# A Fourier mixing layer feeding a mixture of experts: earlier zeroing and sign multiplies, and result scatters queued separately

## The chip, the cores and the metric

The kernel runs on one core of a Trainium2 chip. A core has five engines with one instruction queue each: TensorE (PE in the profile; its weight loads are PEld), VectorE (DVE), ScalarE (ACT), GpSimd (POOL) and SyncE (SP), and 16 DMA engines that move data between the device memory and the core's own memory. An engine takes its instructions in order, and one that waits for a semaphore holds up all that stand behind it in its queue. The metric is the time of one execution on the device in microseconds (us); smaller is better.

## The reference

```python
# x: (8, 2496, 256), filt_r and filt_i: (1249, 256)
X = np.fft.rfft(x, axis=1)
Y = X * (filt_r + 1j * filt_i)[None]
x = np.fft.irfft(Y, n=2496, axis=1).reshape(19968, 256)
logits = x @ w_gate                       # (19968, 8)
expert_idx = np.argmax(logits, axis=1)
probs = softmax(logits)                   # with 1e-9 added to the sum
gate_w = probs[np.arange(N), expert_idx]
for e in range(8):                        # each token goes to one expert
    h = np.maximum(x_of_e @ w1[e], 0.0)   # 256 -> 1024
    y_of_e = h @ w2[e]                    # 1024 -> 256
out = gate_w[:, None] * y                 # in the tokens' own order
```

All is in float32.

## The kernel before, in words

**The Fourier stage.** 2496 is 39 times 64, so a transform is one of length 39 (products with the table `tas`, called stage a), one of length 64 (`tbs`, stage b), a product with the filter `ht`, and the same two backwards (`tcs`, stage c, and `tds`, stage d). A batch is loaded in six chunks of up to four columns (`fin<-in_x`). Stage a's result `zo` goes to the device memory (`zd`) and comes back in another layout (`fin<-zd`); stage c's result `uo` does the same through `ud`. Batch 0 alone is turned on TensorE with transposes (`first_a`, `turn_z`, `first_c`, `turn_u`), without that detour. In `stage_b` VectorE makes three products per pair of frequencies (`ys`, and `yw` in two halves), and for batch 0 and part of the next ones GpSimd adds `yw` to `ys`; otherwise VectorE does.

**The filter and its signs.** `load_filters` loads `ht` in five chunks of four frequencies. The imaginary parts of a chunk are still to be multiplied by signs (`sgs`), on GpSimd. `turn_z` (line 624) issues these multiplies when it reaches a chunk, and has ScalarE copy the real parts to the other half of the partitions.

**The gates.** `logits` or `block_logits` multiply by the gate weights, which lie spread over larger tiles `wg` and `wb` whose other places are zero: `load_rest` (line 435) zeroes each on VectorE and then loads the weights over it from SyncE's queue.

**Routing.** `route` (line 734) finds each token's expert, gate value and place in a list of rows sorted by expert, mostly with small VectorE operations. GpSimd then copies the gate value beside the token's row in `yo`, and `scatter` (line 852) writes 117 rows with one indirect DMA to the table `rows` in the device memory. The tile of `rs`, which holds the gate values, has one buffer, so the next route's `rs` waits until GpSimd has copied the last gate value. `tile_map` (line 866) cuts the list into tiles of rows of one expert.

**The experts.** For a tile of 512, 256 or 128 rows, SyncE loads the rows (`xg`, `ng`) and the two halves of the expert's weights (`w1t`, `w2t`). VectorE transposes the rows. For the larger tiles the first product is done with seven block products in place of eight, for which GpSimd makes sums of weights (`w1_sums`, four operations) and of rows (`turn_x`, four operations). `result` (line 1069) makes 128 rows of the second product from 8 accumulated matmuls, multiplies by the gate on VectorE or ScalarE into one of four `ys` buffers, and has GpSimd write the rows to their places in `out` with an indirect DMA.

**What sets the order.** A class `Order` passes every instruction on and keeps estimated times for each engine while the program is built (`count`, line 178). A loop at the end picks the next piece of TensorE work: a Fourier step, or a product of the experts, whichever is estimated to be ready, in a set proportion. After each pick `flush` (line 490) issues the stores whose data are estimated to be ready, `more_loads` and `prefetch` issue loads, and `side` issues pieces of routing. So an edit that moves an estimate can move other instructions as well. Each engine's order is fixed when the program is built; the semaphore waits are put in by the tile library from reads and writes of the same tile. All instructions go through one line of `Order`, line 243, so the profile names nearly all of them L243, and they are told apart by their tiles.

Of the kernel before, what the change touches and what calls it, by code (L numbers as in the profile page):

```python
# [12 lines left out]
U32 = mybir.dt.uint32  # L13
# [111 lines left out]
class Order:  # L125
# [5 lines left out]
    def __init__(self, nc):  # L131
        self.nc = nc
        self.t = dict.fromkeys(("tensor", "vector", "scalar", "gpsimd", "sync", "transfers"), 0.0)
        self.slow = self.busy = self.last = 0.0
        self.lands = [0.0] * 8
        self.done, self.used, self.slots, self.ahead = {}, {}, {}, {}
        self.tensor, self.vector, self.scalar, self.gpsimd, self.sync = (
            Issue(self, name) for name in ("tensor", "vector", "scalar", "gpsimd", "sync"))
# [37 lines left out]
        return size / n * packet / 14e3 * (1.7 if n >= 1024 and (in_ if out.space == DRAM else out).ap[0][1] <= 64 else 1.0)  # L176

    def count(self, engine, op, args, named):
        aps = [a for a in list(args) + list(named.values()) if isinstance(a, bass.AP)]
        if not aps:  # L180
            return
        out, ins = aps[0], aps[1:]
        if "out" in named:
            out = named["out"]
            ins = [a for a in aps if a is not out]
        if op.endswith("value_load"):
            out, ins = None, aps
        at = named.get("out_offset")
        if at is not None:
            ins.append(at.ap)  # L190
        kept = [a for a in ins if a.space != DRAM or a.name[:2] in ("zd", "ud")]
        free = self.t[engine]
        start = max([free] + [self.ready(a) + (self.HOP if engine != "sync" else 0.0) for a in kept])
        if out is not None:
            start = max(start, self.ahead.pop(out.name, 0.0))
            n = int(np.prod([d[1] for d in out.ap][1:])) if out.space != DRAM else 0
        tail = 0.0
        if op.endswith("dma_start"):
            busy = 1.03 if engine == "gpsimd" else 0.4
            if engine == "sync":  # L200
                start = max(start, self.lands[-8])
            self.t[engine] = start + busy
            took = self.transfer(out, named["in_"])
            self.t["transfers"] = max(self.t["transfers"], start + busy) + took
            end, tail = self.t["transfers"], self.LOAD
            if engine == "sync":
                self.lands = self.lands[-7:] + [end + tail]
        else:
            if out is None:
                took = 0.8 if engine == "sync" else 0.02  # L210
            elif engine == "tensor":
                if start > self.busy + 1.2:
                    self.slow = start + 3.4
                rows = out.ap[0][1]
                took = max(0.1, 0.00085 * n) if op == "transpose" else max(0.216, 0.00169 * n) if rows > 32 else 0.00045 * n
                took *= 2.0 if start < self.slow else 1.0
                tail = 0.25
            elif engine == "vector":
                took = 0.15 + n / 960
            elif engine == "scalar":  # L220
                took = 0.16 + n / 1200
            else:
                took = 0.2 + n / 480
            end = self.t[engine] = start + took
            if engine == "tensor":
                self.busy = end
        for a in kept:
            self.used[a.name] = max(self.used.get(a.name, 0.0), end)
        for key in self.parts(out) if out is not None else ():
            self.done[key] = max(self.done.get(key, 0.0), end + tail)  # L230
        self.last = end + tail
# [59 lines left out]
def kernel(  # L291
# [16 lines left out]
    nc = Order(tc.nc)  # L308
# [39 lines left out]
    tau0 = perm.tile([1, 32], F32, name="tau0")  # L348
# [17 lines left out]
    wg = cst.tile([P, DH, CT], F32, name="wg")  # L366
    wb = cst.tile([P, NJ, CT], F32, name="wb")
# [29 lines left out]
    t = nc.t  # L397
# [17 lines left out]
    signs = []  # L415
# [18 lines left out]

    def load_rest():
        nc.sync.dma_start(out=tds, in_=td)
        nc.vector.memset(wg, 0.0)
        nc.sync.dma_start(out=wg[:, :, :E], in_=moe_w_gate.rearrange("(i p) e -> p i e", p=P))
        nc.vector.memset(wb, 0.0)
        for i in range(4):  # L440
            nc.sync.dma_start(out=wb[i * CT:(i + 1) * CT, :, i * E:(i + 1) * E], in_=moe_w_gate.rearrange("(j p) e -> p j e", p=CT))
        nc.sync.dma_start(out=ids0, in_=ids)
        nc.sync.dma_start(out=vld, in_=valid)

    def make_constants():
        make_identity(nc.nc, ident)
        nc.gpsimd.memset(ones, 1.0)
        nc.gpsimd.affine_select(
            out=tri, in_=ones, compare_op=ALU.is_gt, fill=0.0, base=0, pattern=[[1, P]], channel_multiplier=-1
        )  # L450
        nc.gpsimd.memset(msk, 0.0)
        for i in range(4):
            at = slice(i * CT, (i + 1) * CT)
            nc.gpsimd.tensor_copy(sel[at], ident[at, at])
            nc.gpsimd.memset(msk[at, i:i + 1], 1.0)
        nc.gpsimd.memset(seg, 1.0)
        nc.gpsimd.memset(seg[:, :, 0:1], 0.0)
        nc.gpsimd.memset(tot, 0.0)
        nc.gpsimd.iota(prow, pattern=[[0, 1]], base=0, channel_multiplier=1)
        nc.gpsimd.iota(tau_i, pattern=[[1, 32]], base=0, channel_multiplier=0)  # L460
        nc.vector.tensor_copy(tau0, tau_i)
        nc.gpsimd.iota(e_i, pattern=[[1, E]], base=0, channel_multiplier=0)
        nc.vector.tensor_scalar(em8, in0=e_i, scalar1=-float(E), scalar2=None, op0=ALU.add)
        nc.vector.tensor_scalar(eoff, in0=e_i, scalar1=float(TE), scalar2=None, op0=ALU.mult)
        nc.vector.tensor_copy(cnt, eoff)
        nc.vector.tensor_copy(done, eoff[0:1, :])
        nc.vector.memset(one, 1.0)
# [11 lines left out]
    NIN, YB = 7, 6  # L479
    sb.live["in"] = lambda: {tile.name for tile in ins.values()}  # L480

    moves, stored = [], set()

    def move(o, i):
        moves.append((i, lambda: nc.sync.dma_start(out=o, in_=i)))
# [4 lines left out]
    def flush():  # L490
        while moves and (moves[0][0] is None or nc.ready(moves[0][0]) <= t["tensor"] + 0.2):
            moves.pop(0)[1]()

    def fin(key):
        ins[key] = sb.tile([P, 4, D], F32, tag="in", name="fin", bufs=NIN)
# [128 lines left out]
    def turn_z(f):  # L624
        if f % 4 == 0:
            nc.scalar.copy(out=ht[HP:, f:f + 4], in_=ht[:HP, f:f + 4])
            while signs and signs[0][0] <= f // 4:
                _, part, sign = signs.pop(0)
                nc.gpsimd.tensor_tensor(part, part, sign, op=ALU.mult)
        zi = outs["zi", f] = pro.tile([P, 2, D], F32, tag="zi", name="zi")  # L630
        p = bank().rearrange("p (i h d) -> p i h d", i=2, h=DH)
        for i in range(2):
            for h in range(DH):
                nc.tensor.transpose(p[:, i, h, :], zu["z"][:, h, f + i].rearrange("p t c -> p (t c)"), ident)
        evac(zi, p.rearrange("p i h d -> p i (h d)"), 2 * D)
# [214 lines left out]
            yield  # L850

    def scatter(key, at, what):
        sc = nc.gpsimd.indirect_dma_start(
            out=rowsd,
            out_offset=bass.IndirectOffsetOnAxis(ap=at, axis=0),
# [10 lines left out]
    def tile_map(b, rows, n, last):  # L866
# [19 lines left out]
        yield 3  # L886
        most = max(m for group in GROUPS for _, m in group)
        tau = pools["moe"].tile([1, most], F32, tag="tau", name="tau", bufs=1)[:, :n]
        past = pools["moe"].tile([P, D], F32, tag="ys", name="past", bufs=4)[0:1, :n * (E - 1)].rearrange("p (n e) -> p n e", e=E - 1)
        she = (1, n, E - 1)  # L890
        nc.vector.tensor_tensor(
# [177 lines left out]
    def result(i, j):  # L1069
# [6 lines left out]
        for k in range(FT):  # L1076
            w2 = late["w2s"][:, bass.ds(ev, 1), k, :] if i >= PLACE else w2t[2 * i + k // FH2][:, k % FH2, :]
            mm(p[:, :D], lhsT=hs[i][k % 4 // 2][:, k // 4, k % 2, j * P:(j + 1) * P], rhs=w2, start=(k == 0), stop=(k == FT - 1))
        ys = pools["moe"].tile([P, D], F32, tag="ys", name="ys", bufs=4)
        gate = gis[i][:, j, 8:9]  # L1080
        either(p, D, lambda: nc.vector.tensor_scalar(ys, in0=p[:, :D], scalar1=gate, scalar2=None, op0=ALU.mult),
               lambda: nc.scalar.activation(ys, p[:, :D], AF.Copy, scale=gate))
        nc.gpsimd.indirect_dma_start(
            out=out,
            out_offset=bass.IndirectOffsetOnAxis(ap=gis[i].bitcast(U32)[:, j, :1], axis=0),
            in_=ys,
            in_offset=None,
            bounds_check=N - 1,
            oob_is_err=False,
        )  # L1090


    sides = []
# [199 lines left out]
    def rare_tiles():  # L1293

        for i in range(NT - RARE, NT):
# [4 lines left out]
            for h in (2 * i, 2 * i + 1):  # L1300
                for a in range(4):
                    hidden(i, h % 2, a)
            result(i, 0)

    def share():

# [5 lines left out]
    with tc.manual_schedule(engines=None):  # L1312
# [35 lines left out]
        while fs or any(heads):  # L1348
# [34 lines left out]
            prefetch()  # L1383
            if used["x"] > SHORT and "need" not in late:
                late["need"] = nc.values_load(need, min_val=0, max_val=GROUPS[-1][-1][1])
        with tc.If(late["need"] > GROUPS[-1][-1][1] - RARE):  # L1386
            rare_tiles()

# [29 lines left out]
```

## Time and profile before

| | us |
|---|---|
| median of three runs | 1496.89 |
| lowest, highest | 1492.83, 1498.1 |
| profiled execution, its own time | 1495.25 |
| its span, from the first to the last instruction | 1493.5 |
| TensorE busy | 1456.2 |
| GpSimd busy | 732.0 |
| VectorE busy | 767.1 |
| ScalarE busy | 471.5 |
| mean granted TensorE clock | 0.989 |

The time of an execution is a little longer than the span of its instructions. A group's line in the profile reads: line, engine, operation, what it writes and reads, shape and count; then its busy time and the mean of one in nanoseconds; then the idle time of that engine just before, and what ended it. In a timeline a line gives the start in us, the duration, the engine (SPq is SyncE's queue issuing a DMA), the operation and its tiles; in brackets stands the idle time before it and its releaser. A matmul of 512 float32 columns appears as two passes, so its count is twice the number of instructions in the program. Where a wait is for several semaphores, the releaser named is the one that came last by the profile; if that engine had long been done, it was another.

### The profile page before, as it was taken

What the parts mean: (1) busy time and instruction counts of PE and PEld (TensorE: products, weight loads), DVE (VectorE), ACT (ScalarE), POOL (GpSimd) and SP (SyncE); (2) the same over time, 40 slices, a digit from 0 to 9 for tenths busy, and PEclk for the clock granted to TensorE, in tenths of its full rate; (3) what the DMA queues carried; (4) which work ended last, traced back from release to release, by engine and by line L of the source; (5) the groups of instructions that cost most, each with busy time, mean ns of one, the idle gap of its engine ahead of it and who ended that gap; (6) DMA issues with size and microseconds to landing.
All of it is one profiled execution on the core that took longest, in us unless ns stands there. A gap on an engine that the chain in (4) does not pass through costs nothing. (4 is left out here: it accounts for less than half of the span.)

```text
span 1493.5 us, 24437 instructions
## 1 busy us (share of the span) xinstructions
PE 1456.2 (98%) x7396; PEld 1149.4 (77%) x7396; DVE 767.1 (51%) x1731; ACT 471.5 (32%) x984; POOL 732.0 (49%) x1053
## 2 busy tenths in 40 slices
PE   8898999999999999999999999999999999999998
PEld 6453556767677767777778788887888889999997
DVE  4567669255765665567756545437344344441110
ACT  4454542333332233322222322222222222223332
POOL 3434455355545554555466565664546455741111
PEclk9899999999999999999999999999999999999999
DMA  9649898787875576547355535545455543356661
GB/s 262 203 150 326 288 324 265 229 272 224 293 213 175 153 266 179 161 130 251 106 138 167 176 113 143 125 150 150 149 178 172 170 146 107 112 190 178 182 180 51
DMA packets 216376, 278.10 MB, mean 186 GB/s; under 512 B 124131, under 2 KB 163708, under 8 KB 216245
## 3 DMA queue, kind: packets, MB, share of 16 engines
q1 hardware_dynamic: 197125, 233.19, 52.4%
q0 software_dynamic: 19120, 43.33, 8.4%
q8 instruction: 62, 1.02, 0.3%
q14 instruction: 69, 0.57, 0.1%
HBM read 196.45 MB, written 80.64 MB: 186 GB/s over the span
## 5 line engine op out<-in xcount | busy, mean ns | idle before, releaser
L243 PE MATMUL bank<-w2t,hT 128*128 128x256 f32 x1984 | 446.4, 381 | 1.0 <-DVE hT L243 1.0
L243 DVE TENSOR_TENSOR hT<-bank,hT 128x512 f32<-128x512 f32 (+1 forms) x504 | 300.9, 626 | 277.9 <-PE bank L243 157.8
L243 PEld LDWEIGHTS bank<-w2t,hT 128*128 128x128 f32 x1984 | 376.2, 191 | 64.2 <-issue 10.6
L243 POOL DMA_INDIRECT out_dram<-ys,ng x161 | 160.7, 998 | 473.4 <-ACT ys L243 181.0
L243 PE MATMUL bank<-xT,w1t 128*128 128x256 f32 (+1 forms) x1728 | 316.6, 329 | 0.0
L243 PEld LDWEIGHTS bank<-xT,w1t 128*128 128x128 f32 x1728 | 267.2, 192 | 30.8 <-issue 6.5
L243 ACT ACTIVATE hT<-hT 128x1024 f32<-128x1024 f32 (+1 forms) x144 | 134.6, 960 | 375.1 <-DVE hT L243 364.1
L243 POOL DMA_INDIRECT rows<-yo,row x176 | 180.5, 1026 | 68.5 <-POOL yo L243 28.7
L243 ACT ACTIVATE ys<-bank,ng 128x256 f32<-128x256 f32 x121 | 57.4, 474 | 365.3 <-PE bank L243 311.0
L243 PE MATMUL bank<-sums,wsum 128*128 128x256 f32 (+1 forms) x576 | 135.7, 358 | 0.0
L243 PE MATMUL bank<-w2s,hT 128*128 x592 | 132.6, 379 | 0.0
L243 PEld LDWEIGHTS bank<-w2s,hT 128*128 128x128 f32 x592 | 110.3, 190 | 13.8
L243 PEld LDWEIGHTS bank<-sums,wsum 128*128 128x128 f32 x576 | 100.9, 190 | 20.0 <-issue 9.6
L243 DVE TENSOR_TENSOR ys<-bank,ht 128x512 f32<-128x512 f32 x80 | 54.9, 686 | 64.4 <-PE bank L243 59.8
L243 PE MATMUL bank<-fin,tas 117*120 117x512 f32 x154 | 77.7, 624 | 10.5 <-DMA fin<-in_x_dram 9.9
L243 DVE STREAM_TRANSPOSE xT<-xg 128x512 f32<-128x512 f32 (+2 forms) x126 | 57.5, 495 | 57.1 <-PE bank L243 56.1
L243 PE MATMUL bank<-fin,tds 120*128 120x512 f32 (+1 forms) x168 | 74.9, 565 | 4.3 <-DMA fin<-ud 4.1
L243 PE MATMUL bank<-ys,tcs 128*128 128x512 f32 x140 | 73.9, 613 | 4.1 <-DVE yw L243 3.4
L243 POOL TENSOR_TENSOR wsum<-w1t 128x256 f32<-128x256 f32 x72 | 53.6, 745 | 48.6 <-PE bank L243 45.7
L243 PE MATMUL bank<-fin,tbs 128*128 128x512 f32 x140 | 73.4, 611 | 2.0 <-DMA fin<-zd 2.0
L243 ACT ACTIVATE hT<-bank 128x128 f32<-128x128 f32 (+1 forms) x191 | 57.7, 304 | 53.0 <-PE bank L243 45.0
L243 PE MATMUL bank<-xT,wsum 128*128 128x256 f32 (+1 forms) x288 | 68.9, 362 | 1.9 <-DVE hT L243 1.9
(150 smaller groups left out, 1492.7 us busy)
## 6 DMA issues: line engine op xcount, KB each, us to landing
w1t<-in_moe_w_dram SPq DMA_DIRECT2D x126, 512.0 KB
w2t<-in_moe_w_dram SPq DMA_DIRECT2D x68, 512.0 KB
fin<-in_x_dram SPq DMA_DIRECT2D x39, 512.0 KB
fin<-zd SPq DMA_DIRECT2D x35, 512.0 KB
ud<-uo SPq DMA_DIRECT2D x35, 512.0 KB
fin<-ud SPq DMA_DIRECT2D x35, 512.0 KB
zd<-zo SPq DMA_DIRECT2D x35, 480.0 KB
xg<-rows SPq DMA_DIRECT2D x112, 128.0 KB
```

The costliest lines, as they stand in the source:

```text
L243: return real(*args, **named)
```

## The change

The two memsets of the gate tiles move from `load_rest` to the head of `make_constants`. The sign multiplies of a filter chunk are issued when `turn_z` reaches the chunk before it. A result's scatter is no longer issued at once: `deliver` puts it in a list, and `send` issues it from `flush` when its `ys` is estimated to be ready, or when more than three are waiting; the list is emptied before `tile_map` takes a `ys` buffer and at the end. The result scatters are declared independent of each other in `out`. A flag `sent` tells whether GpSimd's last instruction was an indirect DMA; if so, a one-element memset is issued ahead of the next scatter, in `scatter` and `send`.

```diff
     def count(self, engine, op, args, named):
+        if engine == "gpsimd":
+            self.sent = op == "indirect_dma_start"
...
     def load_rest():
         nc.sync.dma_start(out=tds, in_=td)
-        nc.vector.memset(wg, 0.0)
         nc.sync.dma_start(out=wg[:, :, :E], in_=moe_w_gate.rearrange("(i p) e -> p i e", p=P))
-        nc.vector.memset(wb, 0.0)
...
     def make_constants():
+        nc.vector.memset(wg, 0.0)
+        nc.vector.memset(wb, 0.0)
         make_identity(nc.nc, ident)
...
     def flush():
         while moves and (moves[0][0] is None or nc.ready(moves[0][0]) <= t["tensor"] + 0.2):
             moves.pop(0)[1]()
+        while sends and (nc.ready(sends[0][0]) <= t["tensor"] + 0.2 or len(sends) > 3):
+            send()
...
-            while signs and signs[0][0] <= f // 4:
+            while signs and signs[0][0] <= f // 4 + 1:
...
     def scatter(key, at, what):
+        if nc.sent:
+            nc.gpsimd.memset(tau0[:, 31:], 0.0)
...
     def tile_map(b, rows, n, last):
...
+        while sends:
+            send()
         past = pools["moe"].tile([P, D], F32, tag="ys", name="past", bufs=4)[0:1, :n * (E - 1)].rearrange("p (n e) -> p n e", e=E - 1)
...
     def result(i, j):
...
+        if len(sends) > 3:
+            send()
         ys = pools["moe"].tile([P, D], F32, tag="ys", name="ys", bufs=4)
...
-        nc.gpsimd.indirect_dma_start(
+        deliver(i, j, ys)
+
+    def deliver(i, j, ys):
+        sends.append((ys, gis[i], j))
+
+    def send():
+        ys, ng, j = sends.pop(0)
+        if nc.sent:
+            nc.gpsimd.memset(tau0[:, 31:], 0.0)
+        sc = nc.gpsimd.indirect_dma_start(
             out=out,
-            out_offset=bass.IndirectOffsetOnAxis(ap=gis[i].bitcast(U32)[:, j, :1], axis=0),
+            out_offset=bass.IndirectOffsetOnAxis(ap=ng.bitcast(U32)[:, j, :1], axis=0),
             in_=ys,
             in_offset=None,
             bounds_check=N - 1,
             oob_is_err=False,
         )
+
+        tc.declare_no_dep(sc.ins, group="results", reason="rows of their own")
+        tc.add_to_no_dep_group("results", sc.ins)
```

More of the change, by code (lines that the diff above doesn't have):

```diff
@@ L134, in __init__ @@
         self.slow = self.busy = self.last = 0.0
+        self.sent = False
         self.lands = [0.0] * 8
@@ L480 @@
     sb.live["in"] = lambda: {tile.name for tile in ins.values()}
-    moves, stored = [], set()
+    moves, stored, sends = [], set(), []
     def move(o, i):
@@ L1303, in rare_tiles @@
             result(i, 0)
+            send()
     def share():
@@ L1385 @@
                 late["need"] = nc.values_load(need, min_val=0, max_val=GROUPS[-1][-1][1])
+        while sends:
+            send()
         with tc.If(late["need"] > GROUPS[-1][-1][1] - RARE):
```

## The prediction, made before the changed kernel was run

> **What bounds the kernel now.** I read the page first, then the gaps of TensorE in the timeline, and then, for each gap, the queue of the engine that ended it.
>
> ```profile
> span 1493.5 us, 24437 instructions
> PE 1456.2 (98%) x7396; PEld 1149.4 (77%) x7396; DVE 767.1 (51%) x1731; ACT 471.5 (32%) x984; POOL 732.0 (49%) x1053
> ...
> L243 POOL DMA_INDIRECT out_dram<-ys,ng x161 | 160.7, 998 | 473.4 <-ACT ys L243 181.0
> ```
>
> TensorE is busy for 98% of the span, and its order of work only shuffles pieces of a fixed total. So the change is worth what it takes from the other 2%, 1493.5 - 1456.2 = 37.3 us, and from the stretches at half clock. GpSimd's 473.4 us of idle time before the result scatters is no prize in itself: it costs only where a TensorE gap hangs on it. The table by stages (span, then busy us of PE, PEld, DVE, ACT, POOL, then the granted clock and the DMA share) says where the gaps are:
>
> ```profile
> 0.00:50.00 50.00, 45.72 (x234) 31.71 (x234) 24.33 (x47) 26.24 (x51) 20.85 (x37) 1.00 0.83 234
> 50.00:100.00 50.00, 42.41 (x203) 25.54 (x204) 23.28 (x46) 22.54 (x48) 13.87 (x17) 0.86 0.51 160
> 100.00:150.00 50.00, 44.39 (x130) 19.70 (x130) 38.82 (x82) 21.51 (x46) 24.25 (x40) 0.97 0.94 314
> ...
> 1050.00:1494.00 444.00, 437.43 (x2568) 399.70 (x2566) 138.46 (x310) 122.73 (x286) 180.31 (x240) 1.00 0.50 150
> ```
>
> From 1050 us on nothing is to be had: the 6.6 us missing there are the landing of the last scatter. The worst stage is 50 to 100 us: 7.6 us idle at a clock of 0.86 while the DMA engines are only half busy. TensorE's timeline there, and SyncE's queue:
>
> ```profile
> 48.77 1.06 PE L243 MATMUL bank<-tcs,ys 128*128 128x128 f32 x8
> 56.05 3.74 PE L243 MATMUL bank<-fin,tas 117*120 117x512 f32 x4 [6.23 <-DMA fin<-in_x_dram]
> ...
> 62.12 2.05 PE L243 MATMUL bank<-fin,tbs 128*128 128x512 f32 x2 [0.63 <-DMA fin<-zd]
> ```
> ```profile
> 41.53 0.47 SPq L243 DMA_DIRECT2D tds<-in_td_dram  x1
> 48.44 0.40 SPq L243 DMA_DIRECT2D wg<-in_moe_w_gate_dram  x1
> ...
> 51.78 0.38 SPq L243 DMA_DIRECT2D fin<-in_x_dram  x1
> ```
>
> SyncE stands still from 42.00 to 48.44 because the load of the gate weights waits for VectorE's memset of their tile, which `load_rest` puts behind the filter products in VectorE's order. The x tile that TensorE wants at 49.8 is queued behind it, leaves at 51.78 and lands at 56.05. The second place is near 300 us; GpSimd, VectorE and TensorE in turn:
>
> ```profile
> 292.54 1.01 POOL L243 DMA_INDIRECT out_dram<-ys,ng  x1 [0.30 <-issue]
> 299.49 0.98 POOL L243 DMA_INDIRECT out_dram<-ys,ng  x1 [5.94 <-ACT hT L243]
> ```
> ```profile
> 300.71 0.20 DVE L243 TENSOR_REDUCE rs<-ex 117x6 f32<-117x48 f32 x1 [17.24 <-POOL yo L243]
> ```
> ```profile
> 303.96 0.64 PE L243 MATMUL lt<-yt,wb 128*32 128x128 f32 x16 [2.29 <-DVE yt L243]
> ```
>
> The second scatter's ys was evicted at 294.03, yet it starts at 299.49, 5.94 us after the first was issued: it waits for the first to land in `out`. The last copy of gates queued behind it holds VectorE for 17.24 us, and TensorE pays 2.29 us.
>
> **What the skill says.** "TensorE: Matmul & The Clock Gate", section "What's actually happening": the array falls to half clock after about one idle window of 3.4 us of a free-running activity monitor. The trace agrees, and even shorter gaps can do it: after 6.23 us idle the four passes of fin,tas take 3.74 us instead of 1.88, and after 2.29 us idle the clock record falls too. "DMA: Bandwidth & Descriptors", "Two DMAs through the same engine are not ordered": order comes only from waiting on the completion semaphore. Here that wait is the cost: one result scatter never follows another directly by less than 0.98 + 2.2 = 3.2 us, and needed 7 us at 292. "SBUF — State Buffer", section "SBUF: two separate sides": GpSimd and VectorE share a port under an exclusive lock. At 352 us a VectorE subtraction that usually takes 0.22 us takes 0.75 while a GpSimd sum runs; a GpSimd that no longer waits puts its sums elsewhere, which can move such small losses either way.
>
> **Part 1, the zeroing.** Two memsets (0.11 and 0.27 us) go to the head of VectorE, where it waits 2.27 us for GpSimd's iota anyway: nothing. Removed is SyncE's wait of 6.44 us, so everything behind moves up by that much unless its own data is later. The x load would leave at 51.78 - 6.4 = 45.4 and land 4.27 us later, at 49.6: just in time for 49.8. In the old stretch TensorE spent 49.83 to 67.57 = 17.7 us on work that takes 1.88 + 1.06 + 1.02 + 2.12 + 1.02 = 7.1 us at full clock, so at most 10.6 us are to be had. What is late next is the spectrum tile fin<-zd. Its last store can't go before its eviction, at 46.76, so it leaves near 46.8 to 47.6 against 52.26 to 53.02; 3.6 us until the read is issued (as before) and 4.3 to 5.5 us to land (x's and zd's own times) make 55.5 to 56.7. The new order gives TensorE two tcs groups more ahead of it, so that it arrives at about 54.5: a gap of 1 to 2.2 us, with half clock perhaps (up to 1.7 us more). That leaves 10.6 - (1 to 3.9) = 6.7 to 9.6; I take 8. If the read moves only by 3 us, 4 are left. From 100 to 250 us the DMA share is 0.87 to 0.94, but that work starts earlier by the same amount, and so the gain is kept.
>
> **Part 2, the signs.** VectorE waited 9.1 us in four places for GpSimd's multiply (1.89 us) of the same chunk; now it is done a chunk earlier. TensorE was busy throughout these (only the last falls in its gap), so I count nothing beyond part 1, where it makes the two tcs groups ready. The price: the second chunk's multiply now stands ahead of the first ys sum at 26.59. The scalar copy of that chunk ran at 24.11, and the x load issued just before it at 12.86 was used at 21.51, so it should start by about 24.5 and end by 26.4. If it is 1 us late, TensorE has fin,tas work in hand: 0 to 1, taken as 0.
>
> **Part 3, the scatters.** Removed: the waits of scatter on scatter, and GpSimd's standing still for a ys not yet evicted. Of the TensorE gaps after 250 us only that at 302 is surely behind it: 2.29 us, plus half of the 3.41 us of half clock that follow, 1.7: together 4. The gaps at 365 (0.94) and 426 us (0.77) end on VectorE near such waits, but I don't count them. Those at 683 (1.04, a fin<-ud read), 1013 and 1022 us (1.04 and 1.89, VectorE in `tile_map`) stay. Added: a one-element memset wherever two scatters would meet on GpSimd, 118 of them at 0.1 us (0.09 for the memset of 32x1) = 12 us, up to 0.4 each with the 0.30 us ahead of each scatter = 47. GpSimd is idle for 761 us; without that cover it would be a wait of VectorE or SyncE. A scatter is issued later, behind sums (0.73 each) and row scatters (1.5 with the gap); its buffer of four comes free later. In the tail it waits for its own ys alone, before (1487.94 to 1488.22) and after: nothing. TensorE's order is the same matmuls, 4298 in program order in both.
>
> **Sum.** 8 + 0 + 4 = 12 us off the profiled execution of 1495.25, so 1483.3 by the same measure; the median shown, 1496.89, stands 1.6 above, which makes 1484.9. I say 1485. A measurement of this kernel can tell about 0.5%, 7.5 us, from no change.
>
> **Rivals.**
> *The wait only moves (saves 3 to 7, 1490 to 1494; 0.24).* The read of zd comes no sooner than its store's eviction and a busy queue let it; TensorE idles over 3 us at 53 and half the window is lost again; the reordering near 300 us brings as many small gaps as it removes. For it: 0.63 us of waiting for fin<-zd stands there already. Against it: the DMA engines are half idle at that time.
> *More than counted (saves 16 to 24, 1473 to 1481; 0.14).* The gaps at 244 (3.37 plus half of 6.83 of half clock), 365 and 426 us go as well: 6.8 + 1.7 = 8.5 on top of 12. Against: at 244 VectorE is simply full.
> *Slower (above 1504; 0.07).* A result needs one of four ys buffers. Results come every 3.6 us, so a buffer must be free 14.5 us later; eviction (0.5) and landing (0.98 + 2.2 to 5.6) leave about 8 us for GpSimd's backlog. Behind eight row scatters (8 x 1.5 = 12 us) the eviction would be 4 us late, ScalarE or VectorE stands, the banks fill, and TensorE loses up to 4 + 1.7 us. It decides the sign from about 3 such places, and 1504 is passed at four or five with half the gains. Against: the scatters are let in between the row scatters.
> *No effect (0.05), 1494 to 1500*: the tile library keeps a wait at either place.
>
> **How the numbers follow.** The likeliest case, a saving of 8 to 16 (1481 to 1489), has 0.50. Faster by over 0.5%: 0.50 + 0.14 = 0.64. Within: 0.24 + 0.05 = 0.29. Slower: 0.07. The range leaves out slower (0.07), half of "more than counted" (0.07) and a few hundredths of "no effect": 1476 to 1496.
>
> **What would show it.** Part 1: SyncE's stop at 42 us is gone, the x tile's wait of 6.23 us is under 0.5, a gap of 1 to 3 us before fin,tbs at 55, and the clock of 50 to 100 us is about 0.93. Part 2: no VectorE wait on GpSimd's ht. Part 3: no scatter waits for a landing, GpSimd's idle time before out_dram falls well below 473 us, VectorE's 17.24 us wait is gone. New waits of ys on out_dram's landing would make the prediction wrong, as would gaps over 3 us before fin,tbs or new ones on VectorE after 250 us.

## The result, and the profile after

The changed kernel takes 1489.51 us (median of 22 runs, 1484.68 to 1497.45) against 1496.11 (22 runs, 1490.21 to 1503.03): the ratio is 0.996, with a 95% interval of 0.9948 to 0.9972. It is 6.6 us faster where 12 were forecast. That lies inside the range of 1476 to 1496, but below the likeliest case, and 0.44% falls in the class "within 0.5%", which had 0.29 against 0.64 for "faster".

The page of the changed kernel: span, busy times, and the groups of result scatters and of weight sums on GpSimd.

```profile
span 1490.0 us, 24583 instructions
PE 1452.9 (98%) x7396; PEld 1147.5 (77%) x7396; DVE 772.0 (52%) x1729; ACT 474.0 (32%) x986; POOL 741.9 (50%) x1171
...
L246 POOL DMA_INDIRECT out_dram<-ys,ng x161 | 160.0, 994 | 318.1 <-ACT ys L246 187.9
...
L246 POOL TENSOR_TENSOR wsum<-w1t 128x256 f32<-128x256 f32 x72 | 53.3, 740 | 139.5 <-PE bank L246 122.1
```

GpSimd's idle time before the result scatters fell from 473.4 to 318.1 us, as forecast. That is 155 us less, but 91 of them only moved to stand before the weight sums (139.5 us against 48.6). Neither number says what TensorE got.

TensorE's timeline and SyncE's queue (SPq) of the changed kernel at the place that was the worst stage:

```profile
52.95 1.94 PE L246 MATMUL bank<-fin,tas 117*120 117x512 f32 x4
54.73 1.05 PE L246 MATMUL bank<-tcs,ys 128*128 128x128 f32 x8
57.45 1.10 PE L246 MATMUL bank<-fin,tbs 128*128 128x512 f32 x2 [1.67 <-DMA fin<-zd]
```
```profile
42.76 0.47 SPq L246 DMA_DIRECT2D tds<-in_td_dram  x1
43.29 1.48 SPq L246 DMA_DIRECT2D wg<-in_moe_w_gate_dram  x1
...
48.80 0.38 SPq L246 DMA_DIRECT2D fin<-in_x_dram  x1
```

SyncE no longer stops at 42 us, TensorE no longer waits 6.23 us for the x tile, and a gap of 1.67 us before `fin,tbs` is left, where 1 to 2.2 was forecast. No VectorE operation waits for `ht` any more. GpSimd's timeline at the second place:

```profile
288.88 1.01 POOL L246 DMA_INDIRECT out_dram<-ys,ng  x1 [0.22 <-issue]
289.87 0.09 POOL L246 MEMSET tau<- 1x1 f32 x1
290.20 0.99 POOL L246 DMA_INDIRECT out_dram<-ys,ng  x1 [0.24 <-ACT zo L246]
```

Two result scatters start 1.32 us apart, so neither waits for a landing, and TensorE's gap of 2.29 us at 302 us is gone. Of the steps named in the forecast one isn't to be seen: VectorE's wait of 17.24 us before `rs` was to be gone, but 12.69 us of it stand there still, earlier in the span:

```profile
277.18 0.20 DVE L246 TENSOR_REDUCE rs<-ex 117x6 f32<-117x48 f32 x1 [12.69 <-issue]
```

TensorE has no gap behind it now, so this doesn't cost. The other steps are as forecast, yet half the gain isn't there. The table by stages of the changed kernel (span, then busy us of PE, PEld, DVE, ACT, POOL, then clock and DMA share) says where to look:

```profile
50.00:100.00 50.00, 47.42 (x237) 26.91 (x236) 28.41 (x54) 27.37 (x57) 19.20 (x26) 1.00 0.59 197
...
250.00:350.00 100.00, 100.00 (x479) 76.42 (x478) 40.33 (x120) 34.08 (x83) 47.88 (x82) 1.00 0.83 254
...
600.00:750.00 150.00, 147.97 (x717) 113.80 (x717) 92.45 (x192) 43.70 (x80) 79.66 (x123) 0.99 0.53 160
750.00:900.00 150.00, 146.82 (x789) 114.74 (x790) 82.70 (x181) 42.28 (x85) 92.69 (x148) 1.00 0.51 149
900.00:1050.00 150.00, 146.92 (x695) 128.01 (x694) 84.98 (x193) 38.91 (x60) 91.15 (x139) 1.00 0.53 147
```

The kernel before, from 600 to 1050 us:

```profile
600.00:750.00 150.00, 148.96 (x732) 115.46 (x731) 102.05 (x206) 42.96 (x80) 81.51 (x117) 1.00 0.55 163
750.00:900.00 150.00, 150.00 (x797) 119.01 (x796) 82.78 (x184) 42.71 (x81) 93.83 (x137) 1.00 0.52 151
900.00:1050.00 150.00, 147.07 (x688) 127.85 (x687) 82.82 (x195) 36.65 (x56) 89.33 (x125) 0.99 0.51 142
```

From 600 to 1050 us TensorE stood idle for 1.04 + 0 + 2.93 = 4.0 us before, and for 2.03 + 3.18 + 3.08 = 8.3 us after. Each has one stretch of 3.41 us at half clock there (from 1024.8 before, from 691.8 after). The forecast had nothing changing there. TensorE and VectorE of the changed kernel at the first of these gaps:

```profile
683.12 1.88 PE L246 MATMUL bank<-fin,tbs 128*128 128x512 f32 x4
...
685.12 1.13 PE L246 MATMUL bank<-sums,wsum 128*128 128x256 f32 x4
686.09 1.03 PE L246 MATMUL bank<-sums,w1t 128*128 128x256 f32 x4
...
689.95 1.10 PE L246 MATMUL bank<-ys,tcs 128*128 128x512 f32 x2 [1.12 <-DVE ys L246]
691.95 2.04 PE L246 MATMUL bank<-xT,wsum 128*128 128x256 f32 x4 [0.91 <-DVE yw L246]
```
```profile
685.59 1.48 DVE L246 TENSOR_TENSOR hT<-bank,hT 128x512 f32<-128x512 f32 x2
686.99 0.68 DVE L246 TENSOR_TENSOR ys<-bank,ht 128x512 f32<-128x512 f32 x1
687.68 0.69 DVE L246 SCALAR_TENSOR_TENSOR yw<-bank,ht 64x512 f32<-64x512 f32 x1
688.39 0.68 DVE L246 TENSOR_TENSOR yw<-bank,ht 64x512 f32<-64x512 f32 x1
689.11 0.69 DVE L246 TENSOR_TENSOR ys<-ys,yw 128x512 f32<-128x512 f32 x1
```

VectorE works without a pause from 682.9 to 692.5: three filter groups of four operations (2.8 us each) and two additions to `hT` (1.48 us) fall together, and TensorE twice has to wait for it.

To follow the loss over the whole run I gave each TensorE record a standard interval to the next, by its form (the 20th percentile over the kernels shown), added these up as "work done", and compared the times at which two profiled executions had done the same work. The lead over the kernel before, in us, for the kernels told of below:

```
work done (us)                    75    250    275    600    900    end
changed kernel                   8.4    5.4   10.3    9.8   -1.7    3.7
changed kernel, once more        8.7    5.9   10.8   11.8    2.3    7.7
zeroing alone                    4.5    1.7    5.8    6.1    6.2    7.9
signs alone                      3.7    4.8    7.3    7.3    7.5    7.5
zeroing and signs               12.7   11.4   14.3   13.8   13.5   15.3
freed scatters alone             1.7   -0.5    3.6    3.4    4.6    6.5
scatter edit whole               0.3   -5.4   -0.5    0.5  -10.1   -4.7
all three, scatters at once     11.5    8.6   12.6   12.9   14.2   16.0
late on GpSimd only             11.6   10.5   14.5   15.2   16.4   18.3
late in the plan only            7.1    5.9   10.8   12.2    2.7    8.0
```

Single executions differ by a few us in the first 50 us of loads, so a row is to be read along its length. Between 250 and 275 lies the gap at 302 us. Freed scatters alone win 4.1 there, but so does zeroing alone, in which the result scatters still wait for one another: its profile has no gap there, although a scatter stands for 4.32 us, and none of the half clock. Zeroing and signs win 2.9, with a gap of 1.02 us. From 250 to the end the three kernels with freed scatters planned at once win 7.0 to 7.8, zeroing alone 6.2, zeroing and signs 3.9. So single profiles don't say what the freeing is worth; that is left to the medians below. GpSimd in the kernel with the zeroing alone:

```profile
295.26 0.98 POOL L243 DMA_INDIRECT out_dram<-ys,ng  x1 [4.32 <-ACT yo L243]
```

And four rows lose over 9 us between 600 and 900 and get some 5 back by the end: those in which the result scatters are planned late. From 600 to the end they lose 4.1 to 6.1 us, while all the others win 0.2 to 3.1.

### The profile page after: what moved, and what is told of

The parts are those of the page before. It is cut to its first block, busy times and chain, and to the rows that moved or that the text cites. A ratio compares the mean times of both kernels' runs of the same rounds, so it can differ in the third digit from the quotient of the medians.

```text
span 1490.0 us, 24583 instructions
## 1 busy us (share of the span) xinstructions
PE 1452.9 (98%) x7396; PEld 1147.5 (77%) x7396; DVE 772.0 (52%) x1729; ACT 474.0 (32%) x986; POOL 741.9 (50%) x1171
## 3 DMA queue, kind: packets, MB, share of 16 engines
q8 instruction: 62, 1.02, 0.3%
## 5 line engine op out<-in xcount | busy, mean ns | idle before, releaser
L246 POOL DMA_INDIRECT out_dram<-ys,ng x161 | 160.0, 994 | 318.1 <-ACT ys L246 187.9
L246 ACT ACTIVATE ys<-bank,ng 128x256 f32<-128x256 f32 x129 | 61.2, 475 | 364.4 <-PE bank L246 313.2
L246 POOL TENSOR_TENSOR wsum<-w1t 128x256 f32<-128x256 f32 x72 | 53.3, 740 | 139.5 <-PE bank L246 122.1
L246 PEld LDWEIGHTS bank<-w2s,hT 128*128 128x128 f32 x592 | 110.3, 190 | 13.8
```

What stands on the lines that cost most here:

```text
L246: return real(*args, **named)
```

## The experiments

"Saves" below is (1 - ratio) x 1496 us, the ratio being to the kernel before on the same chip.

**The zeroing alone.**

```diff
     def load_rest():
...
-        nc.vector.memset(wg, 0.0)
...
-        nc.vector.memset(wb, 0.0)
...
     def make_constants():
+        nc.vector.memset(wg, 0.0)
+        nc.vector.memset(wb, 0.0)
```

> Only the two memsets of the gate tiles are moved to the head; TensorE's, GpSimd's and SyncE's orders are those of the kernel before, instruction by instruction. Theory (SyncE's stop at 42 us is worth some 8 us, but the last two tcs groups still wait for the sign multiply): 5 to 7 us off the time of before, the 6.2 us gap of TensorE at 50 us gone, a smaller one of 2 to 3 us in its place. Rival (the DMA engines take the gain back between 100 and 250 us): under 2 us off at the end, though 5 or more at 100 us.

Ratio 0.9971 (0.9956 to 0.9985): it saves 4.3 us, a little under the 5 to 7 expected. TensorE's timeline:

```profile
50.15 1.95 PE L243 MATMUL bank<-fin,tas 117*120 117x512 f32 x4 [1.91 <-DMA fin<-in_x_dram]
51.93 1.06 PE L243 MATMUL bank<-tcs,ys 128*128 128x128 f32 x8
56.76 2.05 PE L243 MATMUL bank<-fin,tbs 128*128 128x512 f32 x2 [3.77 <-DMA fin<-zd]
```

The wait for the x tile is 1.91 us instead of 6.23, but then one stands at the read of the spectrum, 3.77 us, with 6.8 us of half clock around it (55.8 to 62.6).

**Zeroing and signs.** The same, and in `turn_z`:

```diff
-            while signs and signs[0][0] <= f // 4:
+            while signs and signs[0][0] <= f // 4 + 1:
```

> Memsets at the head and signs one chunk ahead; scatters as before. Theory: 8 to 9 us off at 60 us, of which 7 to 9 reach the end, since TensorE is the bound from there on and its order is as before; so more than the whole change gives (6.6). Rival (the gain is given back between 100 and 250 us, not by the scatters): 3 to 5 us off at the end.

Ratio 0.9929 (0.9904 to 0.9953), 1485.95 us: it saves 10.6 us, above the 7 to 9 expected and more than the whole change. The gap before `fin,tbs` is down to 1.74 us, without half clock.

**The signs alone.**

> Only the filter signs multiplied one chunk ahead; zeroing and scatters as before. Theory (the signs pay only because, once the x tile is early, they make the tcs groups ready that fill TensorE's wait for the spectrum read): the x wait of about 6 us near 50 us stays, and the time is within 2 us of the kernel before. Rival (the signs are worth about 5 us by themselves, as zeroing plus signs measured 5 below zeroing alone): 1489.5 to 1492.5.

Ratio 0.9958 (0.9937 to 0.9979), 1488.8 us: it saves 6.3 us. My theory missed; the rival's number is nearer. TensorE's timeline:

```profile
51.86 1.88 PE L243 MATMUL bank<-fin,tas 117*120 117x512 f32 x4
53.58 1.06 PE L243 MATMUL bank<-tcs,ys 128*128 128x128 f32 x8
57.61 3.58 PE L243 MATMUL bank<-fin,tas 117*120 117x512 f32 x4 [2.98 <-DMA fin<-in_x_dram]
```

The x load still leaves late (SyncE stops from 44.75 to 49.40), but the wait for it is 2.98 us instead of 6.23, and half clock there lasts 3.4 us instead of 13.7. So the 9.1 us that VectorE had spent waiting for `ht` were not free: two of the three `tcs,ys` groups that the kernel before had left for after the x tile are done ahead of it. The edit does two things here, though: the waits are gone, and the planner, which now takes these groups to be ready earlier, also puts them ahead in TensorE's order. The two were not taken apart.

**The scatters freed of each other, nothing else.** The order on every engine is that of the kernel before, without the one-element memsets.

```diff
-        nc.gpsimd.indirect_dma_start(
+        sc = nc.gpsimd.indirect_dma_start(
...
+        tc.declare_no_dep(sc.ins, group="results", reason="rows of their own")
+        tc.add_to_no_dep_group("results", sc.ins)
```

> Only the waits of result scatters on one another are taken away; all five engines keep the order of before. Theory: VectorE's wait of 17.2 us at 300 us and TensorE's gap of 2.3 us behind it are gone, 3 to 5 us off at the end, GpSimd's idle time before the result scatters falls little (it still stands before a ys not yet evicted). Rival (the late queue, not the freedom, removes that wait): 0 to 1 us off, the gap at 302 us stays.

Ratio 0.9975 (0.9963 to 0.9987): it saves 3.7 us. VectorE's wait before `rs` was expected to go, but 14.29 us of it stay; TensorE's gap behind it is gone. GpSimd's timeline at the place of the 5.94 us wait, which is now 2.45 us and ends with its own `ys`:

```profile
291.35 1.00 POOL L243 DMA_INDIRECT out_dram<-ys,ng  x1 [1.56 <-ACT ys L243]
294.80 0.98 POOL L243 DMA_INDIRECT out_dram<-ys,ng  x1 [2.45 <-ACT ys L243]
```

**The scatter edit whole**: late queue, freed scatters and memsets, with zeroing and signs as before.

> All of the scatter edit (late queue, freedom, small memsets), zeroing and signs as before. Theory (the new order of TensorE after 280 us costs about as much in new gaps between 600 and 950 us as the freedom gains at 302 us): within 2 us of before. Rival (the scatter edit is worth 4 us and the first two edits lose theirs later): 3 to 5 us off.

Ratio 0.9996 (0.9977 to 1.0014): nothing. Since the freeing alone saves 3.7, the rest of the edit costs about 3.

**All three gains without the late queue.** Zeroing, signs and freed scatters, each scatter issued where the kernel before issues it.

> Zeroing first, signs a chunk ahead, result scatters free of each other, but every scatter issued where the kernel before issues it; no late queue, no one-element memsets. Theory (the gains add, and the late queue alone gives some of them back): 10.6 from zeroing and signs plus 3.7 from the freed scatters = 14.3 us under the kernel before, 1481 to 1484, faster than the changed kernel by 6 to 9 us. Rival (the gains share the same waits, so that 6 to 8 us is all there is, with or without the late queue): 1488 to 1490.

Ratio 0.9916 (0.9896 to 0.9936), 1481.31 us: it saves 12.6 us, and is faster than both kernels. The sum expected, 10.6 + 3.7 = 14.3, lies in the interval of 9.6 to 15.6, but so does 10.6: that the freed scatters bring their full 3.7 us here too is not shown.

**The changed kernel, sending at once.** The memsets stay (105 of them in the profile).

```diff
     def deliver(i, j, ys):
         sends.append((ys, gis[i], j))
+        send()
...
             result(i, 0)
-            send()
```

> The changed kernel with each result scatter sent at once where its ys is made, in the place of being queued late: the freed scatters and 107 one-element memsets between neighbouring scatters stay, and TensorE, VectorE, ScalarE and SyncE have the order of the kernel with zeroing and signs alone. Theory (the memsets are hidden in GpSimd's idle time): as the kernel with the three gains and no memsets, within 1.5 us, some 14 us under the kernel before. Rival (the memsets with their 0.1 us and the gap ahead of the next scatter are what costs the lost half): 6 to 9 us above the kernel without them, near the changed kernel's 1489.5.

Ratio 0.9915 (0.9893 to 0.9938): it saves 12.7 us. The memsets cost nothing and bring nothing that this can tell; all that differs from the changed kernel is when a scatter is sent.

**The changed kernel once more**, beside these two.

> The changed kernel beside the others, to compare within one call. Theory: 6 to 7 us under the kernel before, and 6 to 9 above the two kernels that send their scatters at once. Rival (the lost half is in the parts and not in the queue): level with those two within 2 us.

Ratio 0.9951 (0.9931 to 0.997): it saves 7.3 us, 5.4 less than the two that send at once. The gaps of 1.12 and 0.91 us near 688 and of 0.48 and 1.03 near 866 come again to the hundredth: they belong to the order, not to one execution. One of 1.43 us at 896 doesn't come again, so TensorE is idle for 6.6 us from 600 to 1050 here, not 8.3. That is 4.1 us more than in either kernel that sends at once (2.54 us), and half of the 3.41 us at half clock, which they don't have there, makes 1.7: together 5.8, about the 5.4 that the times differ by.

**The late queue with the wait kept.** The order of the changed kernel on all engines, but without the two `no_dep` lines.

> The changed kernel with the same order on every engine, only the declaration that result scatters don't depend on each other left out, so that 53 of them wait for the landing of the one before. Theory (the freeing is worth 3 to 4 us in the late order too, since VectorE's routes hang on GpSimd behind waiting scatters): 3 to 5 us slower than the changed kernel, 1492.5 to 1494.5. Rival (a scatter that is queued late finds the one before landed already, so that in this order the wait no longer matters): within 1 us of the changed kernel.

Ratio 1.0009 (0.9992 to 1.0026): as slow as the kernel before, 8.0 us over the changed kernel by the medians. I had expected 3 to 5. In this order the freeing is worth more. The profile has a gap of 2.76 us before `fin,tbs` at 256.8 and one of 3.07 in place of 1.61 at 987, each with 3.41 us of half clock after it.

**Late on GpSimd, or late in the plan?** Sending late does two things: GpSimd gets the scatter later, and `Order`, which counts it later, picks another order for the other engines. Two kernels part these. In the first, `count` is told of the scatter at once (`planned`), and GpSimd gets it late (`issue`). `nc.nc` is the engine without `Order`'s count. The memset goes uncounted likewise, by a flag `real` that tells whether the last instruction GpSimd really got was an indirect DMA:

```diff
     def deliver(i, j, ys):
         sends.append((ys, gis[i], j))
...
+        planned(ys, gis[i], j)
+
+    def planned(ys, ng, j):
+        was = nc.real
+        nc.count("gpsimd", "indirect_dma_start", (), dict(out=out, out_offset=bass.IndirectOffsetOnAxis(ap=ng.bitcast(U32)[:, j, :1], axis=0), in_=ys))
+        nc.real = was
+
+    def issue(ys, ng, j):
+        if nc.real:
+            nc.nc.gpsimd.memset(tau0[:, 31:], 0.0)
+        sc = nc.nc.gpsimd.indirect_dma_start(
...
+    def send():
+        issue(*sends.pop(0))
```

> The planner is told of each result scatter where its ys is made, but GpSimd gets it late, by the changed kernel's rule: TensorE, VectorE, ScalarE and SyncE have the order of the kernel that sends at once, and GpSimd alone has the late scatters. Theory (what costs the lost half is the order that the planner gives TensorE and VectorE when it counts GpSimd's scatters later): 1481 to 1484, 12 to 15 under the kernel before, level with the kernel that sends at once. Rival (the scatters' own lateness costs: ys buffers come free later, or row scatters and sums stand behind a batch of result scatters): 1487 to 1490, level with the changed kernel.

In the second, GpSimd gets it at once, and `count` is told late; `planned` and `issue` are as above:

```diff
     def deliver(i, j, ys):
         sends.append((ys, gis[i], j))
...
+        issue(ys, gis[i], j)
...
+    def send():
...
+        planned(*sends.pop(0))
```

> The opposite: GpSimd gets each result scatter at once, but the planner is told of it late, by the changed kernel's rule, so that TensorE, VectorE, ScalarE and SyncE have the changed kernel's order. Theory (the order costs): 1487 to 1490, 6 to 8 under the kernel before, level with the changed kernel, with its gaps near 688 and 867 us. Rival (lateness on GpSimd costs): 1481 to 1484, and those gaps gone.

The first: 1480.22 us, ratio 0.9908 (0.9874 to 0.9941), saves 13.8. The second: 1486.58 us, ratio 0.9939 (0.9914 to 0.9965), saves 9.1. By the traces, TensorE, VectorE, ScalarE and SyncE have the order of the kernels that send at once in the first, and that of the changed kernel in the second; on TensorE the two orders part at 275 us. The intervals, which hold the spread of the kernel before as well, overlap, but the runs themselves hardly do: five of the six of the first are faster than all eight of the second. The traces show where the time goes. The first by stages:

```profile
600.00:750.00 150.00, 150.00 (x736) 116.36 (x734) 100.75 (x203) 42.23 (x79) 81.04 (x124) 1.00 0.54 160
750.00:900.00 150.00, 150.00 (x813) 120.56 (x813) 89.02 (x203) 42.89 (x83) 91.09 (x148) 1.00 0.53 152
900.00:1050.00 150.00, 147.46 (x689) 128.43 (x688) 76.73 (x175) 36.03 (x53) 89.82 (x137) 1.00 0.51 146
```

TensorE of the second, at the places of the changed kernel's gaps:

```profile
687.75 1.10 PE L246 MATMUL bank<-ys,tcs 128*128 128x512 f32 x2 [1.34 <-DVE ys L246]
689.76 2.05 PE L246 MATMUL bank<-xT,wsum 128*128 128x256 f32 x4 [0.91 <-DVE yw L246]
```
```profile
864.96 0.41 PE L246 MATMUL bank<-oe,tri 128*128 128x64 f32 x2 [0.48 <-DVE oe L246]
...
866.62 0.64 PE L246 MATMUL lt<-yt,wb 128*32 128x128 f32 x16 [1.03 <-DVE yt L246]
```

From 600 to 1050 us TensorE is idle for 2.54 us in the first, exactly as in the two kernels that send at once, and for 2.25 + 1.50 + 3.08 = 6.8 us in the second. The gaps go with the plan, whether or not GpSimd is late.

What the order did can be seen beside the kernel with all three gains at once, whose TensorE has a like piece of work some 9 us earlier:

```profile
676.41 1.02 PE L243 MATMUL bank<-fin,tbs 128*128 128x512 f32 x2
677.27 3.62 PE L243 MATMUL bank<-w2t,hT 128*128 128x256 f32 x16
680.82 0.26 PE L243 MATMUL bank<-rx,sel 128*32 128x16 f32 x8
681.01 1.13 PE L243 MATMUL bank<-ys,tcs 128*128 128x512 f32 x2
```

There a result (`w2t,hT`, 3.62 us, which asks VectorE for one operation of 0.48 at most) stands between the filter step and the `ys,tcs` that needs its outcome. In the changed kernel's order two block products of the first layer stand there, 2.2 us in all, whose outcome VectorE has to add to `hT`.

**Another rule for the late queue.**

```diff
-        while sends and (nc.ready(sends[0][0]) <= t["tensor"] + 0.2 or len(sends) > 3):
+        while sends and (nc.ready(sends[0][0]) <= t["tensor"] + 1.5 or len(sends) > 3):
```

> The changed kernel with 1.5 us in place of 0.2 in the queue's rule, so that a result scatter is let in up to 1.3 us of TensorE's time before its ys is done: nothing else is edited, but the planner's order on TensorE and VectorE differs again from about 70 us on. Theory (any such new order is a fresh draw of some tens of small gaps, neither better nor worse on principle): somewhere from 1481 to 1493, its gaps in other places than the changed kernel's 688 and 867 us. Rival (late scatters cost by their lateness): a little better than the changed kernel, 1485 to 1488, with the gaps near 688 and 867 us kept but shorter.

Ratio 0.9976 (0.9962 to 0.999), 1492.34 us: it saves 3.6, just within the range expected, which was wide. By the profile, TensorE's order parts from the changed kernel's at 275 us, later than expected. The gaps are elsewhere, the largest 3.48 us before `oe,tri` at 693, and the stage from 600 to 750 us has 7.9 us of idle time:

```profile
600.00:750.00 150.00, 142.13 (x680) 106.94 (x678) 92.56 (x192) 40.63 (x75) 76.89 (x121) 0.98 0.51 154
```

So 1.3 us in one estimate moved the time by 2.4 to 3.7 us against the changed kernel's two measurements; the intervals overlap, so this is hardly clear of noise. It went to the worse, so this is one more draw and no proof that draws go both ways.

## Why the prediction was right or wrong

**The total** was too high by 5 us. The gains counted were in fact a little larger, 12.6 to 13.8 in the three kernels that have them all and plan the scatters at once, in place of 12; but a term that the sum didn't have, the new order, took 5 to 8 of it:

```
                          forecast    measured
zeroing                       8       4.3 alone
signs                         0       6.3 alone, zeroing and signs 10.6
scatters freed                4       3.7 alone, 2.0 beside zeroing and signs
one-element memsets           0       0
late order                    0       -5 to -8 (by the kernels compared)
sum                          12       6.6
```

**The step that failed** is "its order of work only shuffles pieces of a fixed total", from which it followed that nothing changes after 302 us but what was listed. The total of TensorE's work is indeed fixed (7396 records in all kernels here), but where the pieces stand decides whether VectorE can follow: the kernels that plan the scatters at once save 12.6, 12.7 and 13.8 us, those that plan them late by the changed kernel's rule 6.0 (by the ratio), 7.3 and 9.1. A sign of being wrong that the forecast gave itself, new gaps on VectorE after 250 us, is there: those at 688, 691, 867 and 868 us. The part on the scatters costed the removed waits and the added instructions, and no new order. That the order differs could be seen beforehand; that it costs 5 to 8 us couldn't be worked out from the profile of before. What could have been done is to give "a new order" a width of its own: the trace of before shows VectorE busy for 102 of the 150 us from 600 to 750, and the gaps of 1.04 and 1.89 us at 1013 and 1022 end on it, so that a few more or fewer of these are some us to either side.

**The zeroing and the signs.** SyncE's stop, the x tile, and what is late next (the spectrum read, 1.67 us) came as worked out; the clock of 50 to 100 us is 1.00, not 0.93, since no half clock followed. The two edits were put at 8 us together and measured 10.6, and this was split wrongly between them. "TensorE was busy throughout these" was the wrong test for the signs: what VectorE's waits hold up while TensorE has other work can be missing at the next place where TensorE runs out of work, here at 50 us. Whether the gain is kept from 100 to 250 us isn't shown: between 75 and 250 us of work the changed kernel's lead falls by 3.0 us and that of zeroing and signs by 1.3, but that of two kernels without either edit falls by 2.2 (freed scatters alone) and 5.7 (scatter edit whole). Without the late order the total would still have been some 13 us, close to the 12 forecast. That is in part luck: the zeroing was put at about twice what it saves alone, and the signs at nothing.

**The scatters.** 4 forecast, 3.7 measured. That it comes from the place named, the gap at 302 us, is not shown: with the zeroing alone this gap is gone as well, though the scatters still wait, so how much of it hangs on them differs from one profile to another. Nothing came of the buffers of `ys`: the kernel that is late on GpSimd alone is as fast as any. So the rival "Slower" is refuted in its mechanism. Of "The wait only moves", the size (3 to 7) is what was measured, and one of its sentences, that the reordering brings as many small gaps as it removes, names the cause, but near 300 us where it happened after 600; its other half, a spectrum gap of over 3 us, is what the zeroing without the signs shows.

**What stays open**: which estimate in `Order` made the picks different. `count` keeps GpSimd's time, and the loop reads it for instance to decide when weight sums may start (`w1_sums`), which fits the idle time that moved to them; it wasn't tried apart.

## What to carry to other kernels

Where an order is planned from estimates, an edit to one engine's instructions can draw a new order for all; cost that as a term of its own, and test it by telling the planner and the engine different things, as two kernels do here. When an edit bundles several gains, measure each alone and all but one: here the kernel without the late queue beats the whole change by about 6 us. An engine's wait that TensorE covers with work in hand need not be free, if TensorE runs out of work soon after.

## What the runs showed of the hardware

Short gaps can cost the clock too, and what decides is how much idle time falls into one stretch of a fixed grid. In each of the 14 profiles of this case the changes of the clock lie whole multiples of 3.41 us apart. I laid this grid over each span and added up TensorE's idle time in every stretch at full clock, the ends of the span left out. All 47 stretches with 1.94 us or more were followed by half clock; of those with less than 1.5 us none was, and of the 34 between, 7 were. In the changed kernel the gaps of 1.12 and 0.91 us, 1.1 us apart, put 1.88 us into one stretch, and 3.41 us of half clock follow (from 691.8; 689.9 in its second profile; and 689.3, after 1.34 and 0.91, in the kernel late in the plan only). In the kernel with the wait kept, a border of the grid parts the like pair into 1.19 and 0.91, and in the changed kernel it parts the gap of 1.67 before `fin,tbs` into 1.15 and 0.52: the clock stays full. The Trainium skill, "TensorE: Matmul & The Clock Gate", section "What's actually happening", gives a free-running window of about 3.4 us, and half clock after at least one idle window. The grid has that length, but a stretch with 1.94 us of idle time was always enough here.

What a wait for landings costs depends on the order around it: taking it out saved 3.7 us where scatters were sent at once, and 8.0 where they were sent late.

VectorE's small routing operations can take over three times as long while GpSimd computes. Of the changed kernel's 105 VectorE operations TENSOR_TENSOR of 128x64 between tiles, fifteen take 0.57 to 0.77 us in place of 0.22 (the median of the others). All fifteen overlap a TENSOR_TENSOR of GpSimd; of the other 90, six do. Near 866 us, VectorE and then GpSimd:

```profile
865.51 0.77 DVE L246 TENSOR_TENSOR ex<-lg,mx 128x64 f32<-128x64 f32 x1
866.20 0.76 DVE L246 TENSOR_TENSOR oh<-oh,em 128x64 f32<-128x64 f32 x1
...
867.44 0.23 DVE L246 TENSOR_TENSOR oe<-idx,em 128x64 f32<-128x64 f32 x1
```
```profile
865.46 0.73 POOL L246 TENSOR_TENSOR w1t<-w1t 128x256 f32<-128x256 f32 x1
866.14 0.73 POOL L246 TENSOR_TENSOR wsum<-w1t,wsum 128x256 f32<-128x256 f32 x1
```

This is the stretch ahead of the gaps of 0.48 and 1.03 us, both of which end on VectorE.
